# Later loads of k behind the crossing of the probabilities, and four small moves beside them

## The chip, the cores and the metric

The kernel runs on one core of a Trainium2 chip. The metric is device time in microseconds (us); the time before is the median of three runs.

The core has a matrix engine (TensorE, PE in the profile, with its weight loads as PEld), a vector engine (VectorE, DVE), a scalar engine (ScalarE, ACT), GpSimd (POOL) and SyncE (SP). Each works through its own instructions in order. Here POOL issues the loads from HBM, SP issues the stores of the output and the transposing DMAs, and all DMAs share 16 DMA engines.

## The reference, cut to what matters

Eight batches of attention with eight heads, 576 rows and a head size of 64, in two steps with 32 packed rows between them, then a layer with a cosine gate:

```python
def sm_attn(qq, kk, vv):                    # softmax attention, scale 1/8
    a = softmax(scale * qq @ kk.T)
    return a @ vv
p_packed = sm_attn(p, k, v)                 # 32 packed rows for each batch and head
out = sm_attn(q, p_packed, p_packed)        # 576 rows for each batch and head
x = out.transpose(0, 2, 1, 3).reshape(4608, 512)
h = x @ w_in                                # 512 -> 2048
return (h * cos(h)) @ w_out                 # 2048 -> 512
```

## The kernel before, in words

**Data.** Everything is multiplied in bf16. `load(n, b)` (n is k, q or v, b the batch) is one DMA from POOL that turns 576 rows of eight heads into bf16 in `bf[n, b]` (tiles kbf, qbf, vbf, 576 KB each as written). For the scores, k and q must lie with the head's dimension on the partitions. `pe_T` does that on PE (eight transposes to a group, three groups to a batch, each group copied out of PSUM). `xbar` does it by a transposing DMA from SP, called a crossing here, into `xT[n, b]` (tiles kT with two buffers, qT with one). The first batches are turned on PE, later ones cross.

**One batch.** `s1(b)` makes the scores of the packed rows against kT (L137) and their exponentials, the probabilities `a1` (L146). These must be transposed too: `a1_pe` does it on PE, `a1_xbar` (L160) by a crossing into `a1T` (one buffer), from batch 3 on. `pp(b)` multiplies a1T with v (L180), `pp_T` transposes the result, `ppw(b, n)` multiplies it with a quarter of w_in (L207) and copies it out as PPW (L87 on VectorE, L85 on ScalarE). `s2(b)` makes the second scores from qT, `sums2` and `normalise` the normalised weights a2n. `h_mm(b, fc)` multiplies PPW with a2n for one of 16 feature blocks (L257), takes the cosine on ScalarE (L261) and multiplies on VectorE into gT (L264). `out_gen` multiplies gT with w_out (L345), copies a chunk of 128 rows out as osb (four buffers) and stores it from SP (L351).

**Order.** It is written by hand. The matmuls of `out_gen` for one batch are filler: `fill(n)` puts n of them between steps of the next batch. `slot(s, hooks, ...)` runs the 16 blocks of `h_mm(s, fc)` with filler between them and with hooks after given blocks. In `slot(2)` and later, the hook `tiled(s)` makes two quarters of PPW and then `pp(s + 1)`, so a1T of batch s + 1 must have landed by then; PE reaches that point of batch 3 at 83.68 us and that of batch 4 at 108.32 us. PSUM has three double banks `psA` that go round between `h_mm`, the transposes and `ppw`, and two banks `ot` for the output.

**Loads.** POOL holds back the loads of a stage by a copy of one element, the gate, that reads a tile which a crossing writes, since a gate can't start before the crossing has landed. At L528 it waits for kT of batch 3, then v3, q3 and k4 are loaded; at L564 for kT of batch 4, then v4, q4, k5; at L588, in the loop over s, for kT of batch s + 2, and after it v, q of s + 2 and k of s + 3.

**Other places that the change touches.** In `slot(1)` the hooks of blocks 8, 9 and 10 turn the three groups of k2 on PE (`tk`). After `normalise(2)`, `rest_ppw` copies the second quarter of batch 2's PPW out in two halves, both on VectorE. The last chunk of the output, `tail_chunk` (L331), is made in two pieces of 256 columns, copied by ScalarE and VectorE, each stored as two halves of rows from SP and ScalarE.

Of the kernel before, what the change touches and what calls it, by code (L numbers as in the profile page):

```python
# [8 lines left out]
FP32 = mybir.dt.float32  # L9
BF16 = mybir.dt.bfloat16  # L10
# [5 lines left out]
def kernel(  # L16
# [66 lines left out]
    def copy(eng, out, in_):  # L83
        if eng is ACT:
            ACT.copy(out=out, in_=in_)  # L85
        else:
            eng.tensor_copy(out=out, in_=in_)  # L87
# [1 line left out]
    def psa(dt=FP32):  # L89
        return psum["A"].tile([128, 2, 512 if dt == FP32 else 1024], dt, name="psA", tag="A")  # L90

    def load(n, b):
        bf[n, b] = bf_pool.tile([TP, H, C * D], BF16, name=n + "bf", tag=n + "bf", bufs=1 if n == "q" else 2)
        G.dma_start(out=bf[n, b], in_=srcs[n][b].rearrange("h (p c) d -> p h (c d)", c=C))

    def xbar(n, b):
        t = xT[n, b] = att_pool.tile([128, H * 3, TP], BF16, name=n + "T", tag=n + "T", bufs=2 if n == "k" else 1)
# [5 lines left out]
    def pe_T(n, b, engs=(V, V, V), groups=(0, 1, 2), own=None):  # L103
        if 0 in groups:
            xT[n, b] = att_pool.tile([128, H * 3, TP], BF16, name=n + "T", tag=n + "T", bufs=2 if n == "k" else 1)
        t = xT[n, b]
        flat = bf[n, b].rearrange("p h x -> p (h x)")
        for i in groups:
            ps = own(BF16) if own else psa(BF16)[:, 0, :]
            for j in range(8):  # L110
                o = 8 * i + j
                nc.tensor.transpose(ps[:, j * TP:(j + 1) * TP], flat[:, o * 128:(o + 1) * 128],  # L112
                                    ident[0:TP, 0:TP])
            copy(engs[i], t[:, 8 * i:8 * i + 8].rearrange("p a x -> p (a x)"),
                 ps[:, 0:8 * TP])
# [4 lines left out]
    def pack_p(b0, b1, flat=None):  # L120
        ng = 2 * (b1 - b0)
        if flat is None:
            flat = psa(BF16).rearrange("p a x -> p (a x)")
        for g in range(ng):
            nc.tensor.transpose(flat[:, g * 128:(g + 1) * 128],
                                p_bf[:, 2 * b0 + g].rearrange("p t d -> p (t d)"), ident)
        V.tensor_copy(out=P2[:, b0:b1].rearrange("p b h n -> p (b h n)"), in_=flat[:, 0:ng * 128])
# [30 lines left out]
    def a1_xbar(b):  # L158
        t = a1T[b] = att_pool.tile([128, 2, C, 128], BF16, name="a1T", tag="a1T")
        nc.sync.dma_start_transpose(out=t.rearrange("p a c x -> p (a c) x"),  # L160
                                    in_=a1[b % 2].rearrange("p a c x -> p (a c x)"))
# [33 lines left out]
    def ppw(b, n, eng=None, own=False, later=False, cuts=((0, 512),)):  # L195
        if b not in PPW:
            PPW[b] = ppw_pool.tile([128, 2, DF], BF16, name="PPW", tag="PPW")
        two = isinstance(eng, tuple)
        if own:
            ps = [bank(), bank()]  # L200
        else:
            t = psa()
            ps = [t[:, 0, :], t[:, 1, :]]
        for x in range(4):
            for y in range(2):
                r = slice(64 * y, 64 * y + 64)
                nc.tensor.matmul(ps[y][32 * x:32 * x + 32, :], ppT[b % 2][r, 0, x, :],  # L207
                                 w_in_bf[r, x, n * 512:(n + 1) * 512], start=True, stop=True)

        def evacuate(cuts=cuts):  # L210
            if own or two:
                for a, z in cuts:
                    for y in range(2):
                        copy(eng[y] if two else eng, PPW[b][:, y, n * 512 + a:n * 512 + z], ps[y][:, a:z])
            else:
                copy(eng or (V, ACT)[n % 2], PPW[b][:, :, n * 512:(n + 1) * 512], t)
        if later:
            return [lambda c=c: evacuate((c,)) for c in cuts]
        evacuate()
# [72 lines left out]
    def h_rest(b):  # L292

        t = psa()
        for fc in range(NFC):
            for y in range(2):
                nc.tensor.matmul(t[:, fc // 8, (fc % 8) * 64:(fc % 8) * 64 + 64],
                                 PPW[b][:, y, fc * 128:(fc + 1) * 128], a2n[b][:, y, 512:576],
                                 start=(y == 0), stop=(y == 1))
        cs = cos_pool.tile([128, 2, 512], BF16, name="cosR", bufs=1)  # L300
        ACT.activation(out=cs, in_=t, func=AF.Sin, bias=PI_HALF)
        j0 = (b % 2) * 64
        V.tensor_tensor(out=joint[b // 2][:, :, j0:j0 + 64],
                        in0=t.rearrange("p a (f x) -> p (a f) x", x=64),
                        in1=cs.rearrange("p a (f x) -> p (a f) x", x=64), op=ALU.mult)
# [18 lines left out]

    def tail_chunk(b, c):
        osb = o_pool.tile([128, DM], FP32, name="osb")
        for i in range(2):
            cols = slice(i * 256, i * 256 + 256)
            ps = O.tile([128, 256], FP32, name="ot", tag="ot")
            for fc in range(NFC):  # L330
                nc.tensor.matmul(ps, joint[b // 2][:, fc, :], w_out_bf[:, fc, cols],  # L331
                                 start=(fc == 0), stop=(fc == NFC - 1))
            copy((ACT, V)[i], osb[:, cols], ps)
            for (a, z, rows), q in zip(pieces_of(b, c), (nc.sync, nc.scalar)):
                q.dma_start(out=rows[:, cols], in_=osb[a:z, cols])

# [25 lines left out]
    def fill(n):  # L362
        while n > 0 and filler:
            next(filler[0][0])
            filler[0][1] -= 1
            if filler[0][1] == 0:
                filler.pop(0)
            n -= 1
# [117 lines left out]
    def slot(s, hooks, keep=0, heavy={}, last=None):  # L486


        left = to_do() - keep
        weight = [1 + heavy.get(fc, (0, 0))[0] for fc in range(NFC)]  # L490
        for fc in range(NFC):
            rest = h_mm(s, fc)
            if fc == NFC - 1 and last:
                last()
            rest()
            quota = (left * sum(weight[:fc + 1])) // sum(weight) - (left + keep - to_do())
            behind = min(quota, heavy[fc][1]) if fc in heavy else quota
            fill(quota - behind)
            while hooks and hooks[0][0] == fc:
                hooks.pop(0)[1]()  # L500
            fill(behind)

    def pw2(b, n, eng=None):
        ppw(b, n, eng)
        ppw(b, n + 1, eng)
# [8 lines left out]
        pp(b + 1, V, own=lambda: own)  # L514
        later[1]()

    def tk(n, b, i):
        return lambda: pe_T(n, b, (ACT, V, ACT), (i,))

    def cross(n, b):  # L520
        return lambda: xbar(n, b)

    osb_eng[0] = ACT
    slot(1, [(2, lambda: pw2(1, 2, (ACT, V))), (4, lambda: h_rest(0)), (6, lambda: pack_p(2, 4)), (8, tk("k", 2, 0)), (9, tk("k", 2, 1)),
             (9, cross("q", 2)), (10, tk("k", 2, 2)), (12, cross("k", 3))], 4, {2: (1, 2), 4: (3, 5)})
    ACT.preload_act_table_set(EXP_SET)
    osb_eng[0] = V
    G.tensor_copy(out=gate, in_=xT["k", 3][0:1, 0, 0:1])  # L528
    load("v", 3)
    load("q", 3)  # L530
    load("k", 4)

    set_filler(1)
    fill(4)
# [7 lines left out]
    pp(2)  # L542
    s1(3)
    a1_xbar(3)
    fill(3)
    pp_T(2)
    recips(3)
# [6 lines left out]
    sums2(2, 0)  # L554
    fill(3)
    sums2(2, 1)
    rest_ppw, = ppw(2, 1, (V, V), later=True)
    fill(2)
    normalise(2)
    ACT.preload_act_table_set(SIN_SET)  # L560
    rest_ppw()
    nc.sync.dma_start_transpose(out=P2[:, 4:B].rearrange("p b (t h) n -> p (b t) (h n)", t=2),
                                in_=p_bf[:, 8:2 * B].rearrange("p g t d -> p (g t d)"))
    G.tensor_copy(out=gate, in_=xT["k", 4][0:1, 0, 0:1])  # L564
    for n, b in (("v", 4), ("q", 4), ("k", 5)):
        load(n, b)
    fill(9)
    osb_eng[0] = ACT
    slot(2, [(6, lambda: tiled(2))], 10, {6: (5, 3)}, lambda: pp_T(3, V))
# [1 line left out]
    for s in range(3, B):  # L571
        nxt = s + 1 < B
        ACT.preload_act_table_set(EXP_SET)
        osb_eng[0] = V
        set_filler(s - 1)
        fill(5)
        s2(s)
        ppw(s, 0, V)
        fill(8)
        if nxt:  # L580
            s1(s + 1)
            ppw(s, 1, V)
            a1_xbar(s + 1)
            xbar("q", s + 1)
            recips(s + 1)
            if s + 2 < B:
                xbar("k", s + 2)
                G.tensor_copy(out=gate, in_=xT["k", s + 2][0:1, 0, 0:1])  # L588
        else:
            for n in range(1, 4):  # L590
                ppw(s, n, V)
        fill(4 if nxt else 6)
        sums2(s, 0)
        fill(5)
        sums2(s, 1)
        normalise(s)
        ACT.preload_act_table_set(SIN_SET)
        fill(13)
        osb_eng[0] = ACT
        for n, b in (("v", s + 2), ("q", s + 2), ("k", s + 3)):  # L600
            if b < B:
                load(n, b)
        if nxt:
            slot(s, [(5, lambda: tiled(s))], 5 if s % 2 else 13, {5: (5, 3)}, lambda: pp_T(s + 1, V))
        else:
            slot(s, [], 5)
# [33 lines left out]
```

## Time and profile before

| what | value |
|---|---|
| median of 3 runs | 246.97 us (246.54 to 247.9) |
| profiled execution, its own time | 247.53 us |
| its span, first to last instruction | 245.7 us |
| what lies around the span | 1.83 us |
| ACT busy, DVE busy | 166.6 us (68%), 162.4 us (66%) |
| loads from POOL (q0), share of the 16 DMA engines | 50.3% of the span |
| crossings and stores from SP (q1) | 35.9% |
| granted clock of TensorE | 1.00 in every stage |

The page counts an engine as busy from an instruction's start to its end; ends of matmuls are modelled. The line of a helper stands for all that call it, so a step is found by its tile and its time. In an answer of the trace, "A <- B: 1.2, 1, 1.2" reads: A stood idle 1.2 us until B was done, once, the longest of them 1.2. In a timeline the columns are start, length, engine, line, operation, tiles and shape; square brackets hold the idle time before and what ended it. A DMA's length there is the time to issue it, not to its landing.

### The profile page before, as it was taken

To read this page: it belongs to the slowest core of one execution; us is meant where nothing else is said; L and a number is where in the kernel's file an instruction comes from. 1 tells how busy PE (TensorE), PEld (TensorE's weight loads), DVE (VectorE), ACT (ScalarE), POOL (GpSimd) and SP (SyncE) were. 2 spreads that over 40 slices of the span, in tenths; PEclk is the share of its full clock that TensorE was granted. 3 is DMA by queue.
4 is the path that set the end of the run, shared out by engine and by line. 5 is a ranking of instruction groups with operands and counts; after the bars stand their busy time and mean duration, and the time that the engine had idled before them with its cause. 6 is when DMAs were issued, how large, how long until landed. Compare 5 with 4: busy or idle time off the path is not lost.

```text
span 245.7 us, 5424 instructions
## 1 busy us (share of the span) xinstructions
PE 232.0 (94%) x2204; PEld 128.4 (52%) x2239; DVE 162.4 (66%) x259; ACT 166.6 (68%) x267; POOL 38.1 (16%) x61
## 2 busy tenths in 40 slices
PE   7989889999999799999999999999999999999993
PEld 3463345566545464556455654656455645665452
DVE  3369987686459687578757875868656878784000
ACT  2359998767478587868786787858796766773110
POOL 8532330210130023004100510030100110011000
PEclk9999999999999999999999999999999999999999
DMA  6999999999789989999999799999292111311123
GB/s 87 204 210 207 204 208 227 200 240 149 167 121 185 215 182 197 215 204 174 163 191 237 134 214 207 189 161 179 56 194 51 37 45 43 85 39 49 54 74 85
DMA packets 63992, 37.37 MB, mean 152 GB/s; under 512 B 36592, under 2 KB 59376, under 8 KB 63968
## 3 DMA queue, kind: packets, MB, share of 16 engines
q0 software_dynamic: 23184, 18.81, 50.3%
q1 hardware_dynamic: 40624, 18.09, 35.9%
q8 instruction: 17, 0.28, 0.5%
q10 hardware_dynamic: 160, 0.13, 0.2%
q14 instruction: 7, 0.06, 0.1%
HBM read 37.22 MB, written 9.44 MB: 190 GB/s over the span
## 4 chain that ended last, share of the span: by engine, by line
PE 80%; DMA 13%; ACT 2%; issue 2%; DVE 1%; DVEq 0%
PE ot L345 45%; PE psA L257 21%; DMA qbf<-in_q_dram 7%; DMA a1T<-a 6%; PE ot L385 3%; PE psA L207 2%; PE psA L137 2%; PE psA L180 1%; PE ot L331 1%; PE psA L233 1%; PE psA L112 1%; ACT kT L85 1%; ACT a L146 1%; PE psA L192 0%; PE psA L170 0%
## 5 line engine op out<-in xcount | busy, mean ns | idle before, releaser
L345 PE MATMUL ot<-w_out_bf,gT 128*128 128x512 bf16 x483 | 127.3, 379 | 2.5 <-issue 2.1
L264 DVE TENSOR_TENSOR gT<-psA,cosT 128x576 bf16<-128x576 f32 x112 | 83.3, 757 | 19.5 <-ACT cosT L261 18.5
L261 ACT ACTIVATE cosT<-psA 128x576 bf16<-128x576 f32 x112 | 72.9, 652 | 24.8 <-PE psA L257 23.0
L257 PE MATMUL psA<-a2n,PPW 128*128 128x288 bf16 x448 | 73.3, 286 | 0.4 <-DVE gT L264 0.2
L345 PEld LDWEIGHTS <-gT 128*128 128x128 bf16 x512 | 48.1, 98 | 39.8 <-issue 4.4
L257 PEld LDWEIGHTS <-PPW 128*128 128x128 bf16 x448 | 43.7, 98 | 30.2 <-issue 0.6
L87 DVE CAST PPW<-psA 128x1024 bf16<-128x1024 f32 (+1 forms) x25 | 26.9, 1092 | 6.6 <-PE psA L207 6.4
L87 DVE COPY osb<-ot 128x512 f32<-128x512 f32 (+1 forms) x14 | 9.4, 670 | 20.6 <-PE ot L331 17.6
L85 ACT COPY osb<-ot 128x512 f32<-128x512 f32 (+1 forms) x23 | 13.2, 574 | 14.3 <-PE ot L345 13.2
L268 POOL COPY joint<-gT 128x512 bf16<-128x512 bf16 x14 | 8.6, 617 | 79.9 <-DVE gT L264 79.9
L243 DVE SCALAR_TENSOR_TENSOR a2n<-a2u,r,lns 128x576 bf16<-128x576 bf16 x16 | 12.4, 815 | 10.7 <-ACT lns L241 10.7
L146 ACT ACTIVATE a<-psA 128x576 bf16<-128x576 f32 x16 | 10.3, 646 | 7.8 <-PE psA L137 7.8
L235 ACT ACTIVATE lns<-psA 128x576 f32<-128x576 f32 x16 | 10.3, 650 | 7.2 <-PE psA L233 6.6
L345 PE MATMUL ot<-w_out_bf,joint 128*128 128x512 bf16 x47 | 12.0, 380 | 0.2
L225 ACT ACTIVATE a2u<-psA,rs 128x576 bf16<-128x576 f32 x16 | 11.0, 736 | 1.6 <-PE psA L137 1.4
L385 PE MATMUL ot<-wz 128*128 128x512 bf16 (+1 forms) x15 | 8.3, 660 | 2.0 <-DVE wz L399 1.7
L85 ACT CAST PPW<-psA 128x1024 bf16<-128x1024 f32 (+1 forms) x7 | 6.1, 891 | 5.8 <-PE psA L207 5.8
L241 ACT ACTIVATE lns<-lns 128x576 f32<-128x576 f32 x16 | 10.0, 674 | 0.0
L207 PE MATMUL psA<-w_in_bf,ppT 64*32 64x512 bf16 x224 | 9.8, 379 | 0.0
L289 DVE TENSOR_TENSOR gT<-psH,cosT 128x512 bf16<-128x512 f32 x15 | 9.3, 684 | 0.4 <-ACT cosT L288 0.4
L288 ACT ACTIVATE cosT<-psH 128x512 bf16<-128x512 f32 x15 | 8.4, 627 | 0.7 <-DVE gT L289 0.4
L588 POOL COPY gate<-kT 1x1 bf16<-1x1 bf16 x3 | 0.5, 181 | 50.8 <-DMA kT<-kbf 50.8
(92 smaller groups left out, 173.5 us busy)
## 6 DMA issues: line engine op xcount, KB each, us to landing
kbf<-in_k_dram POOLq DMA_DIRECT2D x8, 576.0 KB, 13.7
vbf<-in_v_dram POOLq DMA_DIRECT2D x8, 576.0 KB, 7.6
qbf<-in_q_dram POOLq DMA_DIRECT2D x8, 576.0 KB, 10.7
out_dram<-osb SPq DMA_DIRECT2D x24, 192.0 KB, 2.7
out_dram<-osb SPq DMA_DIRECT2D x22, 128.0 KB, 2.5
w_in_bf<-in_moe_w_in_dram POOLq DMA_DIRECT2D x4, 512.0 KB, 16.5
w_out_bf<-in_moe_w_out_dram POOLq DMA_DIRECT2D x4, 512.0 KB, 21.3
out_dram<-osb SPq DMA_DIRECT2D x26, 64.0 KB, 2.1
```

What stands on the lines that cost most here:

```text
L85: ACT.copy(out=out, in_=in_)
L87: eng.tensor_copy(out=out, in_=in_)
L146: ACT.activation(out=a1[b % 2][:, y, :, 0:TP].rearrange("p (e m) x -> p e m x", e=2), in_=ps[y][:, :, 0:HS].rearrange("p e (m x) -> p e m ...
L207: nc.tensor.matmul(ps[y][32 * x:32 * x + 32, :], ppT[b % 2][r, 0, x, :], w_in_bf[r, x, n * 512:(n + 1) * 512], start=True, stop=True)
L225: ACT.activation(out=a2u[b][:, y].rearrange("p (e x) -> p e x", e=2), in_=ps[y][:, :, 0:HS], func=AF.Exp, scale=rs1[b][:, y:y + 1])
L235: ACT.activation(out=lns[b][:, y].rearrange("p (e x) -> p e x", e=2), in_=ps[:, :, 0:HS], func=AF.Ln)
L243: V.scalar_tensor_tensor(out=a2n[b][:, y], in0=a2u[b][:, y], scalar=r1[b][:, y:y + 1], in1=lns[b][:, y], op0=ALU.mult, op1=ALU.mult)
L257: nc.tensor.matmul(ps[:, e, 0:HS], PPW[b][:, y, fc * 128:(fc + 1) * 128], a2n[b][:, y, e * HS:(e + 1) * HS], start=(y == 0), stop=(y == 1))
L261: ACT.activation(out=csv, in_=ps[:, :, 0:HS], func=AF.Sin, bias=PI_HALF)
L264: V.tensor_tensor(out=gT[b][:, fc, :].rearrange("p (e x) -> p e x", e=2), in0=ps[:, :, 0:HS], in1=csv, op=ALU.mult)
L345: nc.tensor.matmul(pss[c], w, w_out_bf[:, fc, :], start=(fc == 0), stop=(fc == NFC - 1))
L385: nc.tensor.matmul(wps, w[:, 0:128], w, start=True, stop=True)
```

## The change

- `load` can take a range of heads. k4 is no longer loaded with v3 and q3, but behind a gate on a1T of batch 3.
- k5, k6 and k7 are loaded in two halves of four heads: the first half where the whole stood, the second behind a gate on a1T of the batch before, ahead of the gate on kT.
- In `rest_ppw` of batch 2, one half is copied by ScalarE instead of VectorE.
- k2's first two groups are turned together after block 8, into the two banks of one `psA`; the third stays after block 10. The copies stay with ScalarE, VectorE, ScalarE.
- The last chunk is made in pieces of 256, 128 and 128 columns, copied by VectorE, ScalarE, VectorE.

```diff
-    def load(n, b):
-        bf[n, b] = bf_pool.tile(...)
-        G.dma_start(out=bf[n, b], in_=srcs[n][b].rearrange("h (p c) d -> p h (c d)", c=C))
+    def load(n, b, h0=0, h1=H):
+        if h0 == 0:
+            bf[n, b] = bf_pool.tile(...)
+        G.dma_start(out=bf[n, b][:, h0:h1], in_=srcs[n][b, h0:h1].rearrange("h (p c) d -> p h (c d)", c=C))
+    def behind(t):
+        G.tensor_copy(out=gate, in_=t)
...
-        for i in range(2):
-            cols = slice(i * 256, i * 256 + 256)
+        for i, (a, z) in enumerate(((0, 256), (256, 384), (384, 512))):
+            cols = slice(a, z)
...
-            copy((ACT, V)[i], osb[:, cols], ps)
+            copy((V, ACT, V)[i], osb[:, cols], ps)
...
-    def tk(n, b, i):
-        return lambda: pe_T(n, b, (ACT, V, ACT), (i,))
+    def tk2():
+        t = psa(BF16)
+        halves = [t[:, 1, :], t[:, 0, :]]
+        pe_T("k", 2, (ACT, V, ACT), (0, 1), own=lambda dt: halves.pop())
...
-    slot(1, [..., (8, tk("k", 2, 0)), (9, tk("k", 2, 1)),
-             (9, cross("q", 2)), (10, tk("k", 2, 2)), (12, cross("k", 3))], ...)
+    slot(1, [..., (8, tk2),
+             (9, cross("q", 2)), (10, lambda: pe_T("k", 2, (V, V, ACT), (2,))), (12, cross("k", 3))], ...)
...
     load("v", 3)
     load("q", 3)
-    load("k", 4)
...
     a1_xbar(3)
+    behind(a1T[3][0:1, 0, 0, 0:1])
+    load("k", 4)
...
-    rest_ppw, = ppw(2, 1, (V, V), later=True)
+    rest_ppw, = ppw(2, 1, (ACT, V), later=True)
...
-    for n, b in (("v", 4), ("q", 4), ("k", 5)):
-        load(n, b)
+    load("v", 4)
+    load("q", 4)
+    load("k", 5, 0, H // 2)
...
             a1_xbar(s + 1)
+            if s + 2 < B:
+                behind(a1T[s + 1][0:1, 0, 0, 0:1])
+                load("k", s + 2, H // 2, H)
             xbar("q", s + 1)
...
-        for n, b in (("v", s + 2), ("q", s + 2), ("k", s + 3)):
-            if b < B:
-                load(n, b)
+        if s + 2 < B:
+            load("v", s + 2)
+            load("q", s + 2)
+        if s + 3 < B:
+            load("k", s + 3, 0, H // 2)
```

More of the change, by code (lines that the diff above doesn't have):

```diff
@@ L90, in psa @@
         return psum["A"].tile([128, 2, 512 if dt == FP32 else 1024], dt, name="psA", tag="A")
-    def load(n, b):
-        bf[n, b] = bf_pool.tile([TP, H, C * D], BF16, name=n + "bf", tag=n + "bf", bufs=1 if n == "q" else 2)
-        G.dma_start(out=bf[n, b], in_=srcs[n][b].rearrange("h (p c) d -> p h (c d)", c=C))
+    def load(n, b, h0=0, h1=H):
+        if h0 == 0:
+            bf[n, b] = bf_pool.tile([TP, H, C * D], BF16, name=n + "bf", tag=n + "bf", bufs=1 if n == "q" else 2)
+        G.dma_start(out=bf[n, b][:, h0:h1], in_=srcs[n][b, h0:h1].rearrange("h (p c) d -> p h (c d)", c=C))
+    def behind(t):
+        G.tensor_copy(out=gate, in_=t)
     def xbar(n, b):
@@ L326, in tail_chunk @@
         osb = o_pool.tile([128, DM], FP32, name="osb")
-        for i in range(2):
-            cols = slice(i * 256, i * 256 + 256)
-            ps = O.tile([128, 256], FP32, name="ot", tag="ot")
+        for i, (a, z) in enumerate(((0, 256), (256, 384), (384, 512))):
+            cols = slice(a, z)
+            ps = O.tile([128, z - a], FP32, name="ot", tag="ot")
             for fc in range(NFC):
@@ L523 @@
     osb_eng[0] = ACT
-    slot(1, [(2, lambda: pw2(1, 2, (ACT, V))), (4, lambda: h_rest(0)), (6, lambda: pack_p(2, 4)), (8, tk("k", 2, 0)), (9, tk("k", 2, 1)),
-             (9, cross("q", 2)), (10, tk("k", 2, 2)), (12, cross("k", 3))], 4, {2: (1, 2), 4: (3, 5)})
+    slot(1, [(2, lambda: pw2(1, 2, (ACT, V))), (4, lambda: h_rest(0)), (6, lambda: pack_p(2, 4)), (8, tk2),
+             (9, cross("q", 2)), (10, lambda: pe_T("k", 2, (V, V, ACT), (2,))), (12, cross("k", 3))], 4, {2: (1, 2), 4: (3, 5)})
     ACT.preload_act_table_set(EXP_SET)
     osb_eng[0] = V
-    G.tensor_copy(out=gate, in_=xT["k", 3][0:1, 0, 0:1])
+    behind(xT["k", 3][0:1, 0, 0:1])
     load("v", 3)
     load("q", 3)
-    load("k", 4)
     set_filler(1)
@@ L563 @@
                                 in_=p_bf[:, 8:2 * B].rearrange("p g t d -> p (g t d)"))
-    G.tensor_copy(out=gate, in_=xT["k", 4][0:1, 0, 0:1])
-    for n, b in (("v", 4), ("q", 4), ("k", 5)):
-        load(n, b)
+    behind(xT["k", 4][0:1, 0, 0:1])
+    load("v", 4)
+    load("q", 4)
+    load("k", 5, 0, H // 2)
     fill(9)
@@ L587 @@
                 xbar("k", s + 2)
-                G.tensor_copy(out=gate, in_=xT["k", s + 2][0:1, 0, 0:1])
+                behind(xT["k", s + 2][0:1, 0, 0:1])
         else:
```

## The prediction, made before the changed kernel ran

> **What bounds the kernel now.** I read the page's first part, then the busy time by stage, then what PE waited for. PE is busy 94% of the span, and by stage it is the bound from 40 us on:
>
> ```profile
> PE 232.0 (94%) x2204; PEld 128.4 (52%) x2239; DVE 162.4 (66%) x259; ACT 166.6 (68%) x267; POOL 38.1 (16%) x61
> ...
> 70.00:84.50 14.50, 12.77 (x158) 6.82 (x138) 9.70 (x14) 10.97 (x16) 0.00 (x0) 1.00 1.27 196
> ...
> 100.00:125.00 25.00, 24.58 (x244) 13.95 (x247) 19.39 (x29) 18.98 (x30) 3.72 (x6) 1.00 1.17 192
> 125.00:151.00 26.00, 25.58 (x248) 14.35 (x251) 18.75 (x28) 20.52 (x32) 3.73 (x6) 1.00 1.12 196
> ```
>
> The first columns are the stretch, its length and PE's busy time. PE loses 0.42 us in each of the late stretches, but 1.73 in 70 to 84.5. The clock is 1.00 in all four, so only idle time of PE can be won, or the end after PE's last matmul. PE's waits name the idle time:
>
> ```profile
> PE psA L180 <- DMA a1T<-a: 1.2, 1, 1.2
> ...
> PE psA L257 <- DVE gT L264: 0.2, 1, 0.2
> ...
> PE psA L112 <- ACT kT L85: 0.2, 1, 0.2
> ```
>
> The timeline places the first, and the same point one batch later, where there is no wait:
>
> ```profile
> 67.43 0.44 PE L137 MATMUL psA<-kT,P 64*32 64x288 bf16 x16
> 69.14 0.77 POOL L94 DMA_DIRECT2D kbf<-in_k_dram  x1
> 69.22 4.94 SPq L160 DMA_TRANSPOSE a1T<-a  x1
> 81.86 0.63 PE L207 MATMUL psA<-w_in_bf,ppT 64*32 64x512 bf16 x16
> 83.68 0.56 PE L180 MATMUL psA<-vbf,a1T 96*32 96x64 bf16 x48 [1.20 <-DMA a1T<-a]
> ...
> 97.66 3.65 SPq L160 DMA_TRANSPOSE a1T<-a  x1
> 107.77 0.63 PE L207 MATMUL psA<-w_in_bf,ppT 64*32 64x512 bf16 x16
> 108.32 0.55 PE L180 MATMUL psA<-vbf,a1T 96*32 96x64 bf16 x48
> ```
>
> From L207 to L180 it is 1.82 us for batch 3 and 0.55 for batch 4: the stall is worth 1.27. The crossing of batch 3 took 14.4 us from issue to landing (83.63), that of batch 4 took 9.8 (107.46, 0.86 ahead of PE). Why so long: between 74 and 80 us the DMA view shows it sharing the engines with the loads, packet against packet:
>
> ```profile
> q0 software_dynamic: 1110, 0.84, 91.8%
> q1 hardware_dynamic: 1052, 0.27, 36.7%
> ```
>
> A load is 768 packets of 768 B, this crossing 1536 of 256 B. v3, q3 and k4 landed at 73.91, 79.05 and 82.94, and the crossing 0.7 after the last.
>
> **k4 behind the crossing.** Removed: 768 load packets in front of a1T of batch 3. It then still runs beside q3, which lands at 79.05 as now. By then some 870 of its packets are gone (1052 in 6 us, 175 a us, for 5 us); 670 are left, and crossings without a load beside them moved 3823 packets in 152 to 157, 765 a us: 0.9 us. I take 80.2 for its landing; bounds are 79.4 (just behind q3) and 83.63 (nothing changes). PE comes at 82.4 or earlier, so the 1.27 us go, unless the upper bound holds.
>
> Added: k4 now starts there, and a chain hangs on it. POOL runs the gate and issues k4 at 80.5 (a gate's load came 0.28 after kT landed at 67.33). The trace has no whole load alone in late stages: k0 at the start took 6.2 us, v3 6.3, v5 7.8 with others behind. I take 6.4, near k0, for the q3 crossing shares only the first part: 86.9 (bounds 86.7 to 88.3). SP waits there to issue the crossing of k4 (before at 83.86); queued behind it on SP are the crossing of the last packed rows P and six stores. kT took 5.0 to 6.2 us, 5.6 at this place: I take 5.3, as no load runs: 92.2 against 89.49. P is issued some 3.1 us after kT and took 3.1: 93.2. s1(4) needs both and now starts at 95.87; with all gains before it at 94.3, so 1.1 us remain. The stores have osb's four buffers: copies at 76.25, 80.51 and 89.10 wait for SP until about 91.4, three of four.
>
> The gate on kT then releases v4 at 93.0 (before: 1.14 after kT landed, 90.63; elsewhere 0.66). From v4's issue to a1T's landing it was 16.02 us at batch 3 and 16.83 at batch 4, with three loads. Now half of k5 is missing, 384 packets, 24 on each of 16 engines; v4, q4 and k5 landed 4.5 and 4.1 us apart, so half a load is worth 1.9 to 2.2. That gives 14.0 to 14.9 after 93.0: a1T of batch 4 lands at 107.0 to 107.9, middle 107.45. PE, with what was won before, arrives at 106.8. So **about 0.65 us come back as a new wait at pp(4)**, bounds 0 and, if every step takes its long value, 4.
>
> [...]
>
> **k5 to k7 by halves.** Three more loads (0.77 us of POOL each) and gates (0.18) on POOL, with only the copies to joint (L268) queued behind, which are needed a batch later. The second half goes out when a1T has landed; no half load is in the trace, so between 3.3 us (the 6.2 of a whole less 2.9 for its 768 packets, at the 803 that passed in 166 to 169 us) and 6.2: I take 4.8, the middle. The crossing of k5 then is issued near 112.6 instead of 107.48 and lands at 118; s1(5) wants it at 122. Stores wait on SP until 116, with osb copies at 101.82, 106.20 and 113.25 outstanding, under four. The next loads move from 114.30 to about 118.6 and a1T of batch 5 to about 133; PE reaches pp(5) at 134.68, or 134 after the gains: 1 us left. For batch 6, 157 against 160.5. Cost zero; cover gone, each us late costs one.
>
> **k2 in two steps.** PE's gap of 0.2 before L112 goes: 0.16 in the gap and, as a matmul's end is modelled 0.16 late (379 ns against 216 from start to start), up to 0.33. But s1(3) starts at 67.43 and kT of batch 3 landed at 67.33, and nothing moves that crossing (issued 61.13, 6.2 us). So at most 0.1 survives.
>
> **A copy by ScalarE.** VectorE is rid of one 0.68 us copy between a2n and gT; ScalarE takes 0.59 between its table load and the first cosine, where it had 0.22 idle, so the cosine moves 0.37 back. gT of block 0 starts near 76.67 instead of 76.85, and of PE's wait for gT at 77.65 (0.16 to 0.33) goes 0.2. Bounds minus 0.33 and plus 0.37.
>
> **Tail.** 16 matmuls of 128 columns were 55 ns apart in the transposes, half of 109 for 256: PE time is the same. The last copy on VectorE falls from 426 ns to the 292 of a 128x128 cast: 0.13. Its stores carry half as much; 128 KB took 2.5 and 64 KB 2.1 us, so 0.0 to 0.2 more. I take 0.2 in all.
>
> **The sum**, on the profiled execution (span 245.7, itself 247.53, 0.56 over the median): minus 0.1, minus 0.2, minus 1.27, plus 0.65, minus 0.2 is minus 1.1 us; I take 0.95 because the small terms are near their upper ends. From the median 246.97 this makes **246.0 us**. About 0.5%, 1.23 us, is what a measurement of this kernel can tell from no change, so the likeliest case lies just inside it.
>
> **Rivals.** (1) The loads are quicker than my rows and a1T of batch 4 lands before 106.8: nothing comes back, minus 1.75, 245.2 us. For it: v7 in an emptier stage took 6.6, and v6 to k7 13.8 us in all against 15.9 for v4 to k5. Against: store traffic at 92 to 97. (2) The late chain wins, slower: k4, kT, P and the loads of batch 4 all hang on a1T of batch 3, each by its landing. It decides once a1T of batch 4 lands after 108.3, 0.9 later than I reckon, and passes the old time by over 1.23 us from 109.8. With 81 for a1T, 7.8 for k4, 6.2 for kT, 1.1 for the gate and 14.9, it lands at 111.4: plus 2.9, 249.9 us; at 109.9, just past the point, it gives 248.4. (3) The change does not do what it says: v3 and q3 alone hold a1T until past 82.4, the stall stays, and only the small terms are left: 246.5 us.
>
> **Chances.** My case 0.42, rival 1 0.40, rival 2 0.10, rival 3 0.08. Faster by over 0.5% is rival 1: 0.40; within 0.5% my case and rival 3: 0.50; slower 0.10. The range reaches from rival 1 with the larger tail, 245.0, to 247.5, which leaves out most of rival 2; my case alone is 245.7 to 246.9.
>
> **What would show it.** Right: the wait of L180 on a1T at 82 is gone, k4 is issued near 80.5, kT lands near 92, and L180 near 107 waits for a1T by 0.2 to 1.1 us; waits of s1(4), s1(5) and pp(5) stay nil. Wrong: a1T of batch 3 past 82, a wait of L137 near 94 for kT or P, an osb copy that waits for a store, or no wait at all near 107, which is rival 1.

## The result, and the profile after

The changed kernel took **247.83 us** (median of 22 runs, 247.06 to 250.93) against 246.91 of the kernel before (22 runs, 246.17 to 248.53). The ratio is **1.0032 [1.0016, 1.0048]**: slower by some 0.8 us, 0.4 to 1.2. This ratio and those below leave out executions more than 1.5% above the fastest of the same kernel; here these are two of the changed kernel's, 250.82 and 250.93.

The profiled execution is the shortest of the 22 (247.06, span 245.3), and the one of before, with 247.53, was 0.6 over its median. By the two spans alone the change would look 0.4 us faster. The waits must be read with that in mind. The first part of the changed kernel's page:

```profile
PE 235.6 (96%) x2255; PEld 128.9 (53%) x2255; DVE 161.9 (66%) x259; ACT 166.9 (68%) x268; POOL 40.3 (16%) x68
```

Its busy time by stage (stretch, length, PE, PEld, DVE, ACT, POOL, granted clock, DMA share, GB/s):

```profile
70.00:84.50 14.50, 14.05 (x164) 7.26 (x163) 9.57 (x16) 11.35 (x17) 0.94 (x2) 1.00 1.16 184
...
100.00:125.00 25.00, 25.00 (x249) 13.89 (x248) 19.44 (x29) 18.94 (x31) 4.40 (x8) 1.00 0.95 164
125.00:151.00 26.00, 26.00 (x252) 14.33 (x251) 18.66 (x28) 20.48 (x32) 4.41 (x8) 1.00 1.04 178
```

In 70 to 84.5 PE still loses 0.45 us. That it seems to have won the 0.42 us of the late stretches is a matter of records: the row of `out_gen` has 512 matmuls here and 483 on the page of before, and a missing one leaves a short gap that is put down to "issue". Another profile of this same changed kernel (experiment 9) has 483 again, and with them 0.42 us of idle time in 125 to 151. So the 0.42 us that I read as idle in each late stretch were missing records, not time that could be won. The waits of PE in the changed kernel:

```profile
PE psA L117 <- ACT kT L85: 1.1, 1, 1.1
...
PE psA L262 <- DVE PPW L87: 0.3, 1, 0.3
...
PE psA L262 <- DVE gT L269: 0.2, 1, 0.2
```

The wait for a1T is gone (L185 is the old L180), at batch 3 and, in this execution, at batch 4 too. In its place the transposes of k2 (L117, the old L112) wait 1.09 us for ScalarE, against 0.16 before. Its timeline around k2, then around the copy by ScalarE, then at the two places of `pp`, then the last copy:

```profile
52.52 0.51 PE L117 MATMUL psA<-ident,kbf 96*128 96x96 bf16 x8
54.11 0.50 PE L117 MATMUL psA<-ident,kbf 96*128 96x96 bf16 x8 [1.09 <-ACT kT L85]
...
76.15 0.58 ACT L85 CAST PPW<-psA 128x512 bf16<-128x512 f32 x1
76.77 0.69 DVE L87 CAST PPW<-psA 128x512 bf16<-128x512 f32 x1 [0.92 <-ACT PPW L85]
77.51 0.65 PE L262 MATMUL psA<-a2n,PPW 128*128 128x288 bf16 x4 [0.27 <-DVE PPW L87]
78.78 0.41 PE L262 MATMUL psA<-a2n,PPW 128*128 128x288 bf16 x2 [0.18 <-DVE gT L269]
...
82.98 0.63 PE L212 MATMUL psA<-w_in_bf,ppT 64*32 64x512 bf16 x16
83.61 0.55 PE L185 MATMUL psA<-vbf,a1T 96*32 96x64 bf16 x48
...
107.70 0.63 PE L212 MATMUL psA<-w_in_bf,ppT 64*32 64x512 bf16 x16
108.25 0.56 PE L185 MATMUL psA<-vbf,a1T 96*32 96x64 bf16 x48
...
241.75 0.29 DVE L87 COPY osb<-ot 128x128 f32<-128x128 f32 x1 [1.31 <-PE ot L336]
```

The same places in the kernel before (k2 with a block of `h_mm` between its groups, the copy, the last copy):

```profile
52.62 0.51 PE L112 MATMUL psA<-ident,kbf 96*128 96x96 bf16 x8
...
53.40 0.65 PE L257 MATMUL psA<-a2n,PPW 128*128 128x288 bf16 x4
...
54.21 0.50 PE L112 MATMUL psA<-ident,kbf 96*128 96x96 bf16 x8 [0.16 <-ACT kT L85]
...
75.05 1.28 DVE L87 CAST PPW<-psA 128x512 bf16<-128x512 f32 x2
...
241.83 0.43 DVE L87 COPY osb<-ot 128x256 f32<-128x256 f32 x1 [17.65 <-PE ot L331]
```

Block 8 of `slot(1)` starts 0.1 earlier than before, and `pp(2)` 0.71 later (67.66 against 66.95): k2 in two steps lost 0.81. VectorE's half of the PPW copy starts 0.04 after ScalarE's half has ended, having waited 0.92 for it, and ScalarE's half could only start when the table load was over at 76.14; before, VectorE made both halves from 75.05 on. The third block of `slot(2)` needs the `psA` that the second half frees, so PE waits for it. PE reaches `pp(3)` at 83.61, hardly before the old 83.68: the stall is gone, and two new waits have taken its place.

### The profile page after: what moved, and what is told of

Read it like the earlier page. It is cut to its first block, busy times and chain, and to the rows that moved or that the text cites. A ratio compares the mean times of both kernels' runs of the same rounds, so it can differ in the third digit from the quotient of the medians.

```text
span 245.3 us, 5509 instructions
## 1 busy us (share of the span) xinstructions
PE 235.6 (96%) x2255; PEld 128.9 (53%) x2255; DVE 161.9 (66%) x259; ACT 166.9 (68%) x268; POOL 40.3 (16%) x68
## 4 chain that ended last, share of the span: by engine, by line
PE 85%; DMA 7%; ACT 4%; DVE 1%; issue 1%
PE ot L350 49%; PE psA L262 22%; DMA qbf<-in_q_dram 7%; PE psA L212 3%; PE ot L390 3%; PE psA L142 2%; PE psA L238 2%; PE psA L185 1%; PE ot L336 1%; PE psA L117 1%; ACT kT L85 1%; ACT a L151 1%; ACT L568 1%; PE psA L197 0%; PE psA L175 0%
## 5 line engine op out<-in xcount | busy, mean ns | idle before, releaser
L350 PE MATMUL ot<-w_out_bf,gT 128*128 128x512 bf16 x512 | 133.8, 379 | 0.0
L87 DVE CAST PPW<-psA 128x1024 bf16<-128x1024 f32 (+1 forms) x24 | 26.3, 1108 | 7.9 <-PE psA L212 6.7
L87 DVE COPY osb<-ot 128x512 f32<-128x512 f32 (+2 forms) x15 | 9.7, 644 | 20.2 <-PE ot L336 17.2
L248 DVE SCALAR_TENSOR_TENSOR a2n<-a2u,r,lns 128x576 bf16<-128x576 bf16 x16 | 12.4, 814 | 10.7 <-ACT lns L246 10.7
L85 ACT CAST PPW<-psA 128x1024 bf16<-128x1024 f32 (+1 forms) x8 | 6.7, 853 | 5.9 <-PE psA L212 5.8
L95 POOL DMA_DIRECT2D kbf<-in_k_dram x11 | 8.1, 733 | 4.3 <-DMA w_in_bf<-in_moe_w_in_dram 1.7
```

Of the source, the lines that this page charges most:

```text
L248: V.scalar_tensor_tensor(out=a2n[b][:, y], in0=a2u[b][:, y], scalar=r1[b][:, y:y + 1], in1=lns[b][:, y], op0=ALU.mult, op1=ALU.mult)
L350: nc.tensor.matmul(pss[c], w, w_out_bf[:, fc, :], start=(fc == 0), stop=(fc == NFC - 1))
```

## Experiments

Theories. One says that the loads do what I forecast, and that the loss is PE's two new waits, which come from PSUM: two users of one `psA` tile. The rival says that the loads lose as well, at `pp(4)`, where the late k4 makes a1T of batch 4 late, and that the delay of PE at k2 only hides it. Four kernels with one part each, or one part undone, tell these apart.

**1. The changed kernel without the k2 edit.**

```diff
-    slot(1, [..., (8, tk2), (9, cross("q", 2)), (10, lambda: pe_T("k", 2, (V, V, ACT), (2,))), ...
+    slot(1, [..., (8, tk("k", 2, 0)), (9, tk("k", 2, 1)), (9, cross("q", 2)), (10, tk("k", 2, 2)), ...
```

> The changed kernel with k2 turned as before (three groups, each in a psA of its own). In the profile of the changed kernel PE waits 1.09 us (1.25 from start to start) at L117 for ScalarE's copy of the first group, where before it was 0.33. Theory 1, the k2 step is what costs: the 0.8 us that PE lost between block 8 of slot(1) and pp(2) come back and stay, so about 0.8 us less than the changed kernel, 0.998 to 1.001 of before; no wait of L185 on a1T over 0.2 us. Theory 2, the later loads cost, in a typical run more than in the one profiled: PE that comes 0.8 us earlier only waits for a1T of batches 4 to 6 instead (they landed 1.1, 0.4 and 1.0 us ahead of PE), and the time stays within 0.3 us of the changed kernel, 1.002 to 1.004 of before, with waits of L185 on a1T of 0.3 to 1 us.

Measured: 247.35 us, ratio to before 1.0005 [0.9982, 1.0029]. Its waits:

```profile
PE psA L185 <- DMA a1T<-a: 1.2, 1, 1.2
```

The wait of 1.1 us at k2 is gone, and 1.16 us of wait for a1T of batch 4 stand at 108.70 (landed 108.66). So both theories hold in part: in this profile the 0.8 us were only moved from k2 to `pp(4)`.

**2. The kernel before with the loads alone changed.**

> The kernel before with only the loads changed: k4 behind the crossing of batch 3's probabilities, k5 to k7 by halves. Theory 1 (the loads do their work, other steps lose): the 1.27 us stall at pp(3) goes and nothing comes back, 0.995 of before, 245.7 us. Theory 2 (the late chain of loads gives the gain back and more): the stall at pp(3) goes, but L185 waits for a1T of batch 4, 5 or 6 by 1 to 2.5 us in all, 1.000 to 1.005 of before.

Measured: median 250.0 us, ratio 1.0036 [1.0004, 1.0069]. PE's waits:

```profile
PE psA L185 <- DMA a1T<-a: 1.7, 1, 1.7
```

a1T of batch 3 landed at 79.08, where PE came at 82.73 without a wait; a1T of batch 4 landed at 109.08, and PE waited. The rival held: the loads alone give back more than they win. The ratio understates it. Six of these 12 executions took 250.28 us or more, and none of the 35 of the kernel before that ran beside them took more than 248.17; the median of all twelve lies 2.9 us above before's 247.06. The last section shows what can make an execution that long.

**3. The kernel before with the k2 edit alone.**

> The kernel before with only k2's first two groups turned in one psA. Theory 1: PE waits 1.1 us for ScalarE's copy at the second group, and reaches s1(3) 0.8 us later, so 1.003 of before, plus 0.8 us; as a1T of batch 3 comes 0.8 later too, the stall at pp(3) may shrink by some of it, down to plus 0.3. Theory 2: the same wait, but the stall at pp(3) takes all of it up: 1.000.

Measured: 247.19 us, 1.0013 [0.9995, 1.0031], and in the waits

```profile
PE psA L112 <- ACT kT L85: 1.1, 1, 1.1
```

In its timeline the groups start at 52.82 and 54.41, 1.59 us apart, and the transposes of one group need 0.34 by the start of the matmul behind them: 1.25 lost, against 0.33 and 0.11 before the second and third group of the kernel before, so 0.81 net. The wait comes with this edit alone. That the ratio shows less than 0.8 us would fit what the same profile shows: a1T of batch 3, landed at 81.35, didn't stall PE, which came at 83.50. PE that comes later has less of a stall to lose, where there is one; a single profile doesn't prove it.

**4. The kernel before with the tail alone.**

> The kernel before with only the last chunk in 256, 128 and 128 columns. From the start of the last matmul to the end of the span it was 4.27 us before and 3.79 in the changed kernel's profile. By the prediction's term minus 0.2 us (0.999 of before); by the two profiles minus 0.45 (0.998); if the difference of the profiles was chance in the landing of the last store, no difference. Both theories on the rest expect the same here.

Measured: 246.68 us, 0.9981 [0.996, 1.0003]. From the start of PE's last matmul to the end of the span it took 3.79 us. All seven profiles of this record with the new tail have 3.76 to 3.79, all seven without it 4.27 to 4.30: 0.49 less, every time. But this profile's own span (244.1) is 1.6 shorter than before's, for a second reason: a1T of batch 3 landed at 81.09 and PE did not wait for it at 82.40, with the attention's code untouched. **The stall that I took for a fixed 1.27 us is not in every execution.**

**5. A version without the two new waits: the tail, and k2's two groups transposed back to back before either copy.** The loads and the PPW copy are as before.

```diff
+        for i in range(2):
+            for j in range(8):
+                nc.tensor.transpose(t[:, i, j * TP:(j + 1) * TP], flat[:, o * 128:(o + 1) * 128], ...)
+        for i, eng in ((0, ACT), (1, V)):
+            copy(eng, ..., t[:, i, 0:8 * TP])
```

> The kernel before with the new tail, and k2's first two groups turned back to back into one psA before either copy starts, so that no transpose waits for a copy from the same tile. Theory 1 (what the two steps lost is the program's own wait between the copy and the second group): the wait of 1.1 us at L117 is gone, the loss of 0.33 us of before at the same place too, of which up to 0.4 us stay as kT of batch 3 landed at 65.7 to 66.4 in the last profiles; with the tail 0.997 of before, 246.2 us. Theory 2 (the k2 step costs by something else, such as ScalarE's and VectorE's order in that stretch): PE still loses 0.5 us or more between L117 and s1(3), 1.000 or more.

Measured: 246.48 us (245.62 to 247.56), **0.9972 [0.9946, 0.9998]**: below the changed kernel's 1.0032, and below the kernel before by an interval that just leaves out 1. The tail alone had 0.9981, so most of the 0.7 us can be the tail's. No wait for k2 is left: from block 8 of `slot(1)` to `pp(2)` it is 14.39 us, and 14.82 in the kernel before. Its profile caught a long execution (247.41), with the stall in it:

```profile
PE psA L180 <- DMA a1T<-a: 1.1, 1, 1.1
...
PE psA L137 <- DMA kT<-kbf: 0.6, 1, 0.6
```

**6. The kernel before with the PPW copy alone.** `ppw(2, 1, (V, V), later=True)` becomes `(ACT, V)`.

> The kernel before with only the copy given to ScalarE in rest_ppw. Theory 1: VectorE's half waits for ScalarE's, since both read one psA, PE loses 0.44 us more at the third block of slot(2), as in the two profiles with this copy (0.78 in all from start to start against 0.33): 1.001 to 1.002 of before where a1T of batch 3 isn't late anyway, 1.000 where it is. Theory 2, the prediction's: 0.999 of before.

Measured: 247.5 us, 1.0013 [0.9989, 1.0037]. Around the copy:

```profile
75.46 0.58 ACT L85 CAST PPW<-psA 128x512 bf16<-128x512 f32 x1
76.08 0.69 DVE L87 CAST PPW<-psA 128x512 bf16<-128x512 f32 x1 [0.92 <-ACT PPW L85]
76.83 0.65 PE L257 MATMUL psA<-a2n,PPW 128*128 128x288 bf16 x4 [0.27 <-DVE PPW L87]
78.09 0.65 PE L257 MATMUL psA<-a2n,PPW 128*128 128x288 bf16 x4 [0.18 <-DVE gT L264]
```

The same two waits as in the changed kernel. From `pp(2)` to `pp(3)`, where no DMA held PE in between, the four profiles with this copy take 15.95 us (three of the changed kernel, and experiment 1) and the six without it 15.53 or 15.54: 0.42 lost.

**7. Without both waits, and k4 by halves too.** The changed kernel with the k2 of experiment 5, the PPW copy as before, and k4's first half loaded with v3 and q3, its second behind the crossing. If k4's length is what makes batch 4 late, this brings it forward.

```diff
     load("q", 3)
+    load("k", 4, 0, H // 2)
...
-    load("k", 4)
+    load("k", 4, H // 2, H)
```

> The changed kernel without the copy by ScalarE, with k2's first two groups turned before either copy, and with k4 by halves too: its first half with v3 and q3, the second behind the crossing. By the theory of the late chain (each load of k that is moved behind a crossing delays the next batch's loads by its own landing): k4's second half lands 2 to 2.5 us earlier than the whole one, kT of batch 4 and the loads of batch 4 too, and a1T of batch 4 lands at 105.5 to 106.5, ahead of PE at 106.8 or by at most 0.3 us late, while that of batch 3 lands at 79 to 80, ahead of PE at 82: 0.995 to 0.997 of before. If the lateness came from the halves (more DMAs, each with its own start) and not from k4: a1T of batch 4 later than 108 and 1.002 or more.

Measured: median 248.96 us, 1.0025 [0.9986, 1.0063]. A miss. By its time and its landing it fits the other branch of the expectation, that the halves are what makes the loads late; experiment 8 speaks against that. The half in front held a1T of batch 3 back to 82.28; the second half, issued at 82.87, landed at 87.79, kT at 92.73 and a1T of batch 4 at 108.63, and PE waited:

```profile
PE psA L185 <- DMA a1T<-a: 1.2, 2, 1.0
```

As I read it, the load that is taken out of one stage stands in the next one: with a DMA share of 0.95 to 1.16, as in the changed kernel's stretches above, the place of a load decides who is late.

**8. k4 behind the crossing, k5 to k7 whole.** This takes the halves away and leaves the move of k4.

> The kernel before with k4 behind the crossing of batch 3's probabilities and nothing else: k5 to k7 are whole, as before. By the theory of the late chain: a1T of batch 4 lands about 2 us later than with the halves (109 in the last profile), near 111, and PE waits for it near 107 by 3 us or more; a1T of batch 5 and 6 are late or near it: 1.010 of before or more. If the halves are what makes the loads late: a1T of batch 4 lands by 107.5 and the time is 0.995 to 1.000.

Measured: 253.13 us (4 executions: 248.93, 251.40 and twice 254.87); the ratio is 1.0109 [1.0036, 1.0181]. The profile is of one of 254.87. a1T of batch 4 landed at 112.70, behind a whole k5 (112.54), and PE waited:

```profile
PE psA L185 <- DMA a1T<-a: 4.6, 1, 4.6
```

A whole k5 puts another half of a load in front of a1T of batch 4. With whole loads the move of k4 costs two to three times as much (1.0109 against 1.0036, or 6.1 against 2.9 us by the medians of all executions), so the halves are not what makes the loads late. What they would bring without the move of k4 was not tried.

**9 and 10. The changed kernel, profiled twice more,** since its first profile is its shortest execution.

> The changed kernel once more, for a second profile, as its first is of its shortest execution. Theory 1 (its steps lose, its loads are in time): as in the first, 1.09 us at L117, 0.27 and 0.18 at the third and fourth block of slot(2), no wait of L185 on a1T. Theory 2 (the late chain takes its part in a typical execution): the same and a wait of L185 on a1T of batch 4 or 5 of 0.3 to 1.5 us, since they landed 1.1 and 0.4 us ahead of PE in the first and landings moved by up to 2 us between profiles.

> The changed kernel a third time, with what each theory expects of the second: by theory 1 no wait of L185 on a1T, by theory 2 one of 0.3 to 1.5 us at batch 4 or 5.

Measured: 247.31 and 250.52 us. In the first, PE stood 0.11 us before `pp(4)` (a1T of batch 4 landed at 108.48). In the second it landed at 110.09:

```profile
110.13 0.64 PE L185 MATMUL psA<-vbf,a1T 96*32 96x64 bf16 x48 [1.79 <-DMA a1T<-a]
```

**11. The kernel before, profiled again.**

> The kernel before once more, for a second profile. If the stall at pp(3) that the prediction took for fixed depends on when kT of batch 3 lands: where that is 66.4 or earlier, a1T of batch 3 lands at 81 to 82 and PE does not wait for it, where it is 66.8 or later, 83.5 to 84 and a wait of about 1 us. If the stall is fixed: 1.2 us in any case.

Measured: 246.78 us. No wait for a1T: it landed at 80.58 and PE came at 82.92. That is the kernel before without the stall on which my forecast was built.

**12. The loads alone, profiled again.**

> The kernel before with only the loads changed, once more, as half of its executions took over 249.7 us. If a long wait for a1T of batch 4 is followed by a stretch at half the granted clock, as after the 4.6 us wait with whole loads (6.8 us at 0.50): where the execution takes over 250, the clock is 0.50 for some microseconds right after the wait of L185 near 107, and PE's matmuls there take twice as long. Where it takes under 249, the wait is under 2 us and the clock stays at 1.00.

Measured: 248.69 us. a1T of batch 4 landed at 109.38, and PE waited 2.07 us, a little more than I had expected. The clock stayed at 1.00, as expected.

## Why the prediction was wrong, step by step

The forecast was 246.0, from 245.0 to 247.5; the median, 247.83, lies above the range. It is within the 0.5% that I had set for no change, but the interval leaves out 1, and a forecast of minus 1 us had the wrong sign.

| step | forecast | by the runs | from |
|---|---|---|---|
| k2 in two steps | -0.1 | +0.81 | `pp(2)` against block 8, twelve profiles |
| copy by ScalarE | -0.2 | +0.42 | `pp(2)` to `pp(3)`, ten profiles |
| stall at `pp(3)` | -1.27 | -0.55 | mean over six profiles |
| wait at `pp(4)` | +0.65 | +0.63 | 0, 0.11 and 1.79 |
| k5 to k7 by halves | 0 | 0 | no wait at `pp(5)` |
| tail | -0.2 | -0.49 | last matmul to the end, fourteen profiles |
| sum | -1.1 | +0.8 | measured +0.8 [0.4, 1.2] |

The rows of k2, the copy and the tail agree between profiles to 0.03 us. Those of the stall and of the wait at `pp(4)` are means over executions that differ by more than 1 us. The wait of 1.79 us stands in an execution of 250.52 us, longer than all but two of the 22, and that execution lost 1.6 us more (last section), which the table leaves out. So it is in part luck that the sum meets the measured value.

**k2: "PE's gap of 0.2 before L112 goes".** This step failed, and it is the largest part of the error. I priced what the edit removes and not what it adds. The first group's copy reads one bank of a `psA` tile while the second group wants to write the other, and the program makes PE wait for the copy (1.09 us). Before, each group had a tile of its own and a block of `h_mm` lay between. From block 8 to `pp(2)` it is 15.63 or 15.64 us in the four profiles with this edit and 14.81 or 14.82 in the eight that turn k2 as before. Experiment 3 shows the wait with this edit alone, experiment 5 that it goes when both groups are written before the first copy.

**The copy: "of PE's wait for gT ... goes 0.2".** The same omission. Both halves read one `psA`, and VectorE's half now waits 0.92 us for ScalarE's, which itself waits for its table load (1.28 us long, over at 76.14). With this copy alone gT of block 0 starts at 77.29, where I had reckoned 76.67. My upper bound of plus 0.37 was passed; I took the wrong end and bounded only ScalarE's delay. The wait could have been read before: in `slot(1)` two quarters of batch 1's PPW are already copied with (ACT, V), and VectorE waits for ScalarE there too.

```profile
43.79 1.07 ACT L85 CAST PPW<-psA 128x512 bf16<-128x512 f32 x2 [0.37 <-PE psA L207]
...
44.41 1.29 DVE L87 CAST PPW<-psA 128x512 bf16<-128x512 f32 x2 [0.20 <-ACT PPW L85]
```

These rows also settle what the wait is for. Each holds one half of each quarter. ScalarE's half of the first quarter ends at 44.38, and VectorE's half of that quarter, from the same `psA`, starts 0.03 later. But ScalarE's half of the second quarter, from another `psA`, runs from 44.27 to 44.87 beside it, into the same tile PPW. So two engines do write one PPW tile at once here, and what keeps the two halves in turn is the `psA` that they share.

**The stall: "the stall is worth 1.27".** The mechanism was right: with k4 away, a1T of batch 3 lands at 77.2 to 79.2 us in six profiles and never holds PE. That is earlier than the 80.2 of the forecast, for q3 did not land "at 79.05 as now" but at 75.89 to 77.58 in the changed kernel: kT landed 0.6 to 1.7 earlier, and without k4 behind it q3 took 9.2 to 9.8 us and not 10.7. a1T landed 1.1 to 1.3 behind q3, as reckoned (1.15). The size was not, for I read one execution as all. Six profiles have the loads of before:

| kernel | kT of b3 landed | a1T of b3 landed | wait of PE |
|---|---|---|---|
| before, second profile | 65.31 | 80.58 | 0 |
| tail alone | 65.67 | 81.09 | 0 |
| k2 edit alone | 66.33 | 81.35 | 0 |
| copy alone | 66.84 | 83.86 | 1.0 |
| before, first profile | 67.33 | 83.63 | 1.2 |
| tail and k2 back to back | 67.75 | 83.92 | 1.1 |

Where kT of batch 3 lands early the stall isn't there; it is worth 0.55 us on average. That the profiled execution lay 0.56 over the median was in front of me, and I used it only to shift the sum.

**The give-back: "about 0.65 us come back as a new wait at pp(4)".** The mechanism, a chain from k4 over kT to the loads and a1T of batch 4, is what the runs show, and the size is near by luck. Two errors cancel in it. PE came at 108.25, not 106.8, because of the waits at k2 and at the copy. And the chain is longer than I made it: k4 alone took 7.5 to 8.1 us where I took 6.4, and from v4's issue to a1T of batch 4 it was 15.2 to 17, not 14.0 to 14.9 (all in the changed kernel's three profiles); a1T of batch 3 landing at 77.16, not 80.2, made up for that in the first one. A slip of mine is small beside this: half of 4.5 and 4.1 us is 2.2 and 2.1, not 1.9 to 2.2. With the loads of before a1T of batch 4 landed at 104.55 to 108.71 (mean of six 106.9), with the new ones at 107.19 to 110.09 (mean of six 108.8): 1.9 later, for 4 us that a1T of batch 3 wins. Without the delay at k2 PE waits 1.16 us there, without that and the one at the copy 1.69 and 2.07. The first profile has no wait at `pp(4)`, which I had named as the sign of rival 1; the sign misled, for PE was late as well. So rival 2 was the right one to fear for the loads: its point, a landing after 108.3, is passed in five of the six profiles, and I gave it 0.10.

**By halves, and the tail.** The second half of k5 took 5.3 us (4.8 taken) and a1T of batch 5 landed at 134.23, 0.4 ahead of PE. The tail won 0.49 where I took 0.2. The traces split it, nearly alike in all profiles that have the landing of the last store: the last copy starts 0.26 after the start of the last matmul and not 0.37 (that matmul has 128 columns and not 256), takes 0.29 and not 0.43, the last store lands 2.08 after its issue and not 2.22, and from there to the end of the span it is 1.11 and not 1.23. I had the second part and the third; the first and the last, 0.1 each, were not in my sum, and why the end follows sooner on the last landing was not tried.

As single parts against before, the ratios are 1.0036, 1.0013, 1.0013 and 0.9981 for loads, k2, copy and tail, some 1.06 us together, and each has an interval of 0.4 to 0.8 us either way; that agrees with the table but proves no single line of it.

**Open.** Why kT of batch 3 lands anywhere from 65.3 to 67.8 us in kernels whose code up to there is the same or nearly so; the early loads differ from execution to execution (the 384 KB load of p took 21.5 us in the first profile of before and 20.7 in the changed kernel's), and no run here isolates it.

## What to carry to other kernels

Before two uses are put into one PSUM tile, look at who reads the first while the second is written: in this kernel the wait follows the tile, not the bank (1.09 us at k2), and two engines that copy halves of one tile follow one another (0.92 us at the PPW copy). Look in the profile of before for a place that already does it. A stall in one profile is worth its mean over several executions (here 0.55 us, from 0 to 1.2); where a DMA's landing decides it, profile twice before pricing it. With the changed kernel's DMA share of 0.95 to 1.16, the loads moved behind one crossing stood in front of the next (a1T of batch 4 landed 1.9 us later on average), so follow the chain until a stage with room.

## What the runs showed of the hardware that I had not expected

Two waits of PE cost more than their own length here. Behind the 1.79 us of experiment 10 the granted clock was 0.50 for 3.41 us; busy time by stretch, granted clock third from the right:

```profile
106.60:110.10 3.50, 1.74 (x22) 0.48 (x20) 1.21 (x2) 1.70 (x3) 0.00 (x0) 1.00 1.36 128
110.43:113.84 3.41, 3.08 (x43) 1.58 (x27) 1.55 (x3) 0.65 (x1) 0.68 (x1) 0.50 0.97 144
113.84:117.00 3.16, 3.16 (x23) 2.13 (x22) 2.41 (x4) 2.17 (x4) 0.00 (x0) 1.00 0.40 64
```

From `pp(4)` to `pp(5)` this execution took 27.97 us, the other two of the same kernel 26.37 and 26.36: 1.6 more. Behind the 4.6 us of experiment 8 the clock was 0.50 for 6.82 us, twice as long, and from `pp(4)` to `pp(5)` it took 29.28 us, 2.9 more:

```profile
112.11:118.93 6.82, 6.18 (x66) 3.27 (x67) 2.77 (x5) 1.30 (x2) 0.30 (x2) 0.50 1.15 208
```

Yet 1.69 and 2.07 us in experiments 2 and 12 left it at 1.00 (26.35 and 26.36 us from `pp(4)` to `pp(5)`). So it isn't the length alone; what else decides was not shown. A wait of 1.69 or 2.07 us at `pp(4)`, with the 1.6 or 2.9 us lost at half the clock behind it, would by my estimate from these numbers make executions as long as the six of experiment 2; only experiments 8 and 10 show such a stretch.
